# Reordering small copies, weight conversions and the mixing steps in a retention, softplus and SwiGLU kernel

## The chip, the cores and the metric

The kernel runs on one core of a Trainium2 chip. The metric is the time of one execution on the device in microseconds (us); lower is better. A core has five engines that run side by side, each through its own instructions in order: TensorE (PE in the rows; its weight loads are PEld), VectorE (DVE), ScalarE (ACT), GpSimd (POOL) and SyncE (SP, which issues most of the DMAs). An instruction that waits holds up everything behind it in its engine's queue, and nothing else.

## What is computed

```
state = gamma * state + k_t v_t^T ;  y_t = scale * q_t state        # retention, 2 x 8 heads, 768 steps, 64 wide
x  = y as [1536, 512]
h  = x @ w_in ; g = max(h, 0) + log1p(exp(-|h|)) ; x = g @ w_out     # 512 -> 2048 -> 512
rms = sqrt(mean(x * x) + 1e-6) ; xn = x / rms * rms_g
out = (silu(xn @ w_gate) * (xn @ w_val)) @ w_out2                    # 512 -> 1536 -> 512
```

Weights arrive as 64-bit floats and are read as pairs of 32-bit words. Every operand of a product is held as a high part (rounded) and a low part (the rest), and a product is three matmuls over these: high by high, high by low, low by high.

## The kernel before, in words

**Tiling.** The 1536 tokens are three blocks of 512, called 0, 1 and 2; block 2 is `LONE`. Features lie in tiles of 128. After retention come four groups of softplus layers: an `l1` piece makes one tile of h for a block (12 matmuls of 128 x 512), an `l2` piece adds one tile of the second layer (12 matmuls). In the last group the `l2` pieces of a block are followed by its norm: squares (ScalarE), sums over features (`sums`, VectorE), a mean by eight small matmuls and twelve small VectorE steps that give the root (`mean`), and four transposes with a ScalarE copy that lay the root along the tokens (`along`). For blocks 0 and 1 the normed x is then scaled (`scaled`) and split into high and low parts (`part`, `part_hi`, `part_lo`); block 2 is scaled only after its product, and its x parts are made by `high` and `low` in `norm`.

**Seven products.** The gate and value layers go in pairs of feature tiles, p = 0 to 5. Blocks 0 and 1 are multiplied together in seven products instead of eight (class `Seven`, p1 to p7, six matmuls each): x of both blocks is mixed into T1 to T4, B11, B21, B22 (`mixing`, eight steps of VectorE and ScalarE), and weights into two sums S (GpSimd, `combine` and `parts`). Bank Q collects p1, p6, p7 and p4, bank R p5 and p3. Between p1 and p6, p6 and p7, p7 and p4 ScalarE copies Q out (`copied`), since the partial value is wanted too; the next product into Q must wait for that copy. Block 2 has plain `l3` products (12 matmuls). Then Silu, the product of gate and value, its split (`to_g`: a high part on ScalarE, a low part on VectorE), and `l4` pieces (six matmuls) into the output.

**Order.** All is issued by hand, piece by piece. A piece's matmuls are issued first; then `piece(after, conv, us)` advances a planned clock by 2.72 or 1.36 us, runs what is due (`run`), what was deferred (`flush`, which also issues one weight load if a staging tile is free), as many conversions as asked, the piece's own `after`, and then one step each of two background lists, `bg` (sums, mean, along, plain, block after block) and `mix` (mixing). The planned clock decides only the order of the instructions. Pieces of the first pair come in the order: four `l2` pieces of block 2, then g.p1, g.p2, v.p1, v.p2 (g is the gate, v the value), four `l3` pieces, and the list of 14 that the last loop spells out. A round of p = 1 to 5 is four `l3` pieces alternating with four `l4` pieces (h0, L0, h1, L1, h2, L2, h3, L3), then two lists of eleven.

**Conversion of a weight tile** (`convert`): two ScalarE steps (`small`, `size`), two VectorE steps (`shift`, `bits`) and a GpSimd sum (`total`); later, by due times, `finish` (VectorE), `high` (ScalarE); for each second tile of gate and value also `combine` (four GpSimd steps), `whole` (two VectorE low parts), `parts` (two ScalarE high parts) and `rest` (two GpSimd low parts). `need` asks for a weight when its product is issued; were it not ready, all that is due would be run at once. There are 12 weight slots and three staging tiles.

## Time and profile before

| | us |
|---|---|
| median of three runs | 632.7 |
| the runs | 632.7, 2134.71, 631.86 |
| the profiled execution | 632.48 |
| its span (first to last instruction) | 630.8 |
| TensorE, VectorE, ScalarE, GpSimd busy | 605.5, 459.3, 355.5, 275.0 |
| granted TensorE clock, mean share | 0.992 |

The profile is of one execution. Busy time is the time with an instruction of that engine under way; 1.7 us of the execution lie outside the span. The granted clock is a share of 2.4 GHz.

### The profile page before, as it was taken

The numbers are of one execution on the slowest core, as the hardware profiler recorded it, in microseconds if no ns is written. First come the engines' busy times: TensorE is split into PE (matmuls) and PEld (weight loads), VectorE is DVE, ScalarE is ACT, GpSimd is POOL, SyncE is SP. The second block draws the span as 40 slices with busy tenths as digits, with TensorE's granted clock in tenths as the row PEclk, the third lists the DMA queues.
The fourth block names the chain that finished last, engine by engine and source line by source line (L and its number), as shares of the span: only waits on it lengthen the run. The fifth ranks groups of instructions, "written<-read, shape, count | busy, mean of one in ns | idle before, by whom it ended". The sixth has DMA issues, their size and how long they took to land.

```text
span 630.8 us, 8631 instructions
## 1 busy us (share of the span) xinstructions
PE 605.5 (96%) x3232; PEld 498.3 (79%) x3232; DVE 459.3 (73%) x655; ACT 355.5 (56%) x612; POOL 275.0 (44%) x228
## 2 busy tenths in 40 slices
PE   9999999999999999999897899899999999999997
PEld 8788888888888888887676678678878878878886
DVE  5787777678734774357879987489789789889735
ACT  3456677787746775566645564744444444543420
POOL 3444254544411442022321477277377377377211
PEclk9999999999999999999988999999999999999999
DMA  9997132333311331111100221211311212220014
GB/s 205 219 233 191 63 94 87 91 98 100 101 33 34 100 101 34 34 34 34 33 1 1 72 96 46 88 59 42 100 38 64 75 59 68 68 67 35 1 51 150
DMA packets 65562, 48.84 MB, mean 77 GB/s; under 512 B 39792, under 2 KB 60528, under 8 KB 65520
## 3 DMA queue, kind: packets, MB, share of 16 engines
q1 hardware_dynamic: 64320, 47.90, 26.9%
q8 instruction: 25, 0.41, 0.3%
q10 hardware_dynamic: 1200, 0.39, 0.2%
q14 instruction: 17, 0.14, 0.1%
HBM read 45.14 MB, written 3.15 MB: 77 GB/s over the span
## 4 chain that ended last, share of the span: by engine, by line
PE 57%; DVE 26%; ACT 8%; issue 4%; POOL 2%; SPq 2%; DMA 1%; DVEq 0%; POOLq 0%; ACTq 0%
PE h L483 18%; PE l L563 15%; PE l L885 6%; PE Q L787 5%; DVE g L765 4%; DVE w L200 3%; DVE a L258 3%; PE y L443 2%; DVE w L196 2%; PE R L787 2%; PE l L540 2%; PE sc L391 1%; DVE ws_w_gate L214 1%; SPq L84 1%; DVE ws_w_val L214 1%
## 5 line engine op out<-in xcount | busy, mean ns | idle before, releaser
L204 POOL TENSOR_TENSOR c<-w,c 128x512 uint32<-128x512 uint32 x68 | 87.8, 1291 | 169.1 <-DVE w L200 127.4
L483 PE MATMUL h<-x,ws_w_in 128*128 128x512 f32 x576 | 138.9, 391 | 0.0
L563 PE MATMUL l<-g,ws_w_out 128*128 128x512 f32 x528 | 129.8, 397 | 1.9 <-DVE g L125 1.9
L483 PEld LDWEIGHTS h<-x,ws_w_in 128*128 128x128 f32 x576 | 107.6, 188 | 22.9 <-issue 0.7
L563 PEld LDWEIGHTS l<-g,ws_w_out 128*128 128x128 f32 x528 | 101.2, 192 | 23.7 <-DVE g L125 2.2
L885 PE MATMUL l<-ws_w_out,g 128*128 128x512 f32 x432 | 109.3, 390 | 2.1 <-DVE g L765 2.1
L885 PEld LDWEIGHTS l<-ws_w_out,g 128*128 128x128 f32 x432 | 81.0, 188 | 20.0 <-DVE g L765 2.8
L521 DVE SCALAR_TENSOR_TENSOR t<-h,t 128x512 f32<-128x512 f32 x48 | 33.1, 690 | 73.9 <-ACT t L514 73.9
L214 POOL TENSOR_TENSOR ws_w_out<-a,ws_w_out 128x512 fp32r<-128x512 f32 x28 | 38.8, 1387 | 50.5 <-ACT ws_w_out L217 50.5
L258 DVE SCALAR_TENSOR_TENSOR a<-a,c 128x512 f32<-128x512 f32 x68 | 52.8, 776 | 9.3 <-POOL c L204 9.3
L124 ACT ACTIVATE g<-t 128x512 fp32r<-128x512 f32 x48 | 30.3, 632 | 37.2 <-DVE t L521 37.2
L765 DVE TENSOR_TENSOR g<-t,g 128x512 fp32r<-128x512 f32 x36 | 41.5, 1176 | 11.1 <-ACT g L764 8.2
L509 ACT ACTIVATE t<-h 128x512 f32<-128x512 f32 x48 | 28.6, 595 | 34.8 <-PE h L483 34.8
L125 DVE TENSOR_TENSOR g<-t,g 128x512 fp32r<-128x512 f32 x48 | 33.8, 707 | 13.0 <-ACT g L124 10.3
L214 POOL TENSOR_TENSOR ws_s<-s,ws_s 128x512 fp32r<-128x512 f32 x24 | 41.0, 1727 | 4.6 <-ACT ws_s L217 4.6
L808 POOL TENSOR_TENSOR t<-t,e 128x512 f32<-128x512 f32 x18 | 27.8, 1544 | 33.9 <-DVE e L804 33.9
L787 PE MATMUL Q<-T,ws_s 128*128 128x512 f32 x144 | 36.9, 394 | 2.7 <-ACT p L793 2.6
L764 ACT ACTIVATE g<-t 128x512 fp32r<-128x512 f32 x36 | 21.5, 624 | 28.6 <-DVE t L865 14.6
L483 PE MATMUL h_w_gate<-x,ws_w_gate 128*128 128x512 f32 x144 | 36.3, 403 | 0.0
L233 POOL TENSOR_TENSOR s<-a 128x256 f32<-128x256 f32 x24 | 21.3, 887 | 32.2 <-DVE a L258 32.2
L915 DVE TENSOR_TENSOR o<-l,o 128x512 f32<-128x512 f32 x39 | 26.6, 684 | 11.3 <-PE l L885 11.0
L787 PEld LDWEIGHTS Q<-T,ws_s 128*128 128x128 f32 x144 | 26.7, 188 | 10.2 <-ACT p L793 4.8
(132 smaller groups left out, 1041.2 us busy)
## 6 DMA issues: line engine op xcount, KB each, us to landing
st_w_out<-in_moe_w_out_dram SPq DMA_DIRECT2D x28, 512.0 KB, 3.4
st_w_in<-in_moe_w_in_dram SPq DMA_DIRECT2D x16, 512.0 KB, 3.8
st_w_gate<-in_moe_w_gate_dram SPq DMA_DIRECT2D x12, 512.0 KB, 3.6
st_w_val<-in_moe_w_val_dram SPq DMA_DIRECT2D x12, 512.0 KB, 3.5
v<-in_v_dram SPq DMA_DIRECT2D x12, 256.0 KB, 4.7
q<-in_q_dram SPq DMA_DIRECT2D x23, 128.0 KB, 4.4
k<-in_k_dram SPq DMA_DIRECT2D x23, 128.0 KB, 3.9
out_dram<-o SPq DMA_DIRECT2D x11, 256.0 KB, 2.0
```

The lines of the kernel that those rows point to most:

```text
L124: nc.scalar.activation(out=hi, in_=src, func=AF.Copy)
L125: eng.tensor_tensor(out=lo, in0=src, in1=hi.bitcast(F32), op=ALU.subtract)
L204: nc.gpsimd.tensor_tensor(out=c, in0=w, in1=c, op=ALU.add)
L214: eng.tensor_tensor(out=out[:, 1], in0=src, in1=out[:, 0].bitcast(F32), op=ALU.subtract)
L258: nc.vector.scalar_tensor_tensor(out=a, in0=a, scalar=TINY, in1=c.bitcast(F32), op0=ALU.is_ge, op1=ALU.mult)
L483: nc.tensor.matmul(h, lhsT=w[:, i, kk * P:(kk + 1) * P], rhs=src[j][kk // 2][:, kk % 2, :], start=(n == 0), stop=(n == 3 * KC - 1))
L509: nc.scalar.activation(out=got[0], in_=h, func=AF.Abs)
L521: nc.vector.scalar_tensor_tensor(out=t, in0=h, scalar=0.0, in1=t, op0=ALU.max, op1=ALU.add)
L563: nc.tensor.matmul(p, lhsT=w[:, i, m * P:(m + 1) * P], rhs=g_t[b, f][:, j, :], start=(n == 0 and f == (0 if keep else fs[0])), stop=(n == ...
L765: nc.vector.tensor_tensor(out=g[:, 1], in0=t, in1=g[:, 0].bitcast(F32), op=ALU.subtract)
L787: nc.tensor.matmul(ps, lhsT=halves(w[:, i], p)[:, kk * P:(kk + 1) * P], rhs=t[j][:, kk, :], start=start and n == 0, stop=n == 5, skip_grou ...
L885: nc.tensor.matmul(ps4, lhsT=g_t[b, f][:, j, m * P:(m + 1) * P], rhs=w[:, i, :], start=n == 0 and (i, j) == TERMS[0], stop=n == 1 and (i, ...
```

## The change

Four things are done. In p1, p6 and p7 the copy of Q becomes the piece's `first`, which `piece` runs ahead of everything else that it issues. The steps of a conversion get later due times, the two sums' tiles are taken in `combine`, and the calls of `convert` stand at other pieces. The last background step of block 0 (`plain`) becomes four, one feature tile each, and the two lists become a list of chains, of which each gives a step per piece: block 0's, block 1's, mixing (seven empty steps ahead), block 2's, in this order. Means and roots of blocks 1 and 2 stand one or two steps later, and the last list of the first pair puts each `l4` piece one place later.

```diff
@@ -207,7 +207,7 @@
         t = rows(slot[key], f"ws_{nm}")
         raw[key] = a
         if gated and f % 2:
-            sums, sa = [], [row(f"s{n}", "s") for n in range(2)]
+            sums, sa = [], []
             reserved[0] += 2
 
         def rounded(out=t, src=a, eng=nc.gpsimd):
@@ -224,6 +224,7 @@
         def combine():
             other = ws[nm, f - 1]
             a0, a1 = raw.pop((nm, f - 1)), a
+            sa.extend(row(f"s{n}", "s") for n in range(2))
             s1, s2 = (halves(sa[0], p) for p in range(2))
             s3, s4 = (halves(sa[1], p) for p in range(2))
             for out, x0, x1, op in ((s1, halves(a1, 0), halves(a1, 1), ALU.add),
@@ -251,7 +252,7 @@
                         rounded(out, sa[n])
                         ready.add(("S", nm, f // 2, n))
                 later(1.4, rest)
-            later(1.3, whole)
+            later(2.6, whole)
             later(4.0, parts)
 
         def finish():
@@ -259,13 +260,13 @@
                                            op0=ALU.is_ge, op1=ALU.mult)
             if not gated:
                 if nm == "w_out2":
-                    later(1.0, last)
+                    later(2.6, last)
                 else:
                     deferred.append(last)
             else:
-                later(1.0, high)
+                later(2.6, high)
                 if f % 2:
-                    later(0.9, combine)
+                    later(1.3, combine)
 
         ws[key] = t
         left[key] = 2 if gated else NB
@@ -284,7 +285,7 @@
         if nm in ("w_in", "w_out"):
             deferred.append(finish)
         else:
-            later(4.0, finish)
+            later(5.4, finish)
         return True
 
     def need(key):
@@ -472,7 +473,7 @@
 
     g_t, acc, tags = {}, {}, {}
     bg = []
-    mix = []
+    chains = []
     LONE = NB - 1
 
     def project(h, w, src):
@@ -636,17 +637,16 @@
             for do in waiting.pop(b, ()):
                 do()
 
-        def plain():
-            scaled(b, range(KC))
-            for m in range(KC):
-                part(("B11", "B21")[m // 2], m % 2, acc[b, m])
+        def plain(m):
+            scaled(b, (m,))
+            part(("B11", "B21")[m // 2], m % 2, acc[b, m])
 
         if m == KC - 1:
-            bg.extend(([None, sums, None, mean, None, along, plain],
-                       [None, sums, mean, along],
-                       [None, sums, None, mean, None, along])[b])
+            chains.append(([None, sums, None, mean, None, along] + [lambda m=m: plain(m) for m in range(KC)],
+                       [None, sums, None, mean, None, None, along],
+                       [None, None, None, sums, None, mean, along])[b])
             if b == 1:
-                mix.extend([None, None, None, None] + mixing())
+                chains.append([None] * 7 + mixing())
 
 
     TB, waiting = {}, {}
@@ -813,8 +813,12 @@
             self.Q = self.hold("Q")
             self.product(self.Q, (self.nm, 2 * self.p), 0, "B11", True)
 
+            def first():
+                self.c1 = self.copied(self.Q, "p1")
+
             def after():
-                self.c1 = self.copied(self.Q, "p1")
+                pass
+            after.first = first
             return after
 
         def p2(self):
@@ -837,17 +841,24 @@
             self.product(self.Q, key, 1, "T2", False)
             free.append(slot[key])
 
+            def first():
+                self.c6 = self.copied(self.Q, "p6")
+
             def after():
-                self.c6 = self.copied(self.Q, "p6")
+                pass
+            after.first = first
             return after
 
         def p7(self):
             self.product(self.Q, ("S", self.nm, self.p, 1), 0, "T3", False)
 
+            def first():
+                self.c7 = self.copied(self.Q, "p7")
+
             def after():
-                t, tag = self.copied(self.Q, "p7")
-                self.added(1, 1, self.R, t)
-                two.append(tag)
+                self.added(1, 1, self.R, self.c7[0])
+                two.append(self.c7[1])
+            after.first = first
             return after
 
         def p4(self):
@@ -922,17 +933,15 @@
 
     def piece(after, conv=1, us=2.72):
         clock[0] += us
+        if hasattr(after, "first"):
+            after.first()
         run()
         flush()
         for _ in range(conv):
             convert()
         after()
-        if bg:
-            step = bg.pop(0)
-            if step:
-                step()
-        if mix:
-            step = mix.pop(0)
+        for chain in chains:
+            step = chain.pop(0) if chain else None
             if step:
                 step()
 
@@ -1112,33 +1121,33 @@
             for n, one in enumerate([g.p1, g.p2, v.p1, v.p2]):
                 piece(one(), n == 1, half)
             for n, one in enumerate(h):
-                piece(one(), n in (1, 3))
+                piece(one(), n in (1, 2))
             later(0.4, gs_of(p, LONE))
             L = l4s(0, LONE)
-            for n, one in enumerate([g.p5, v.p5, g.p6, v.p6, L[0], g.p7, v.p7, L[1], g.p4, v.p4, L[2], g.p3, v.p3, L[3]]):
+            for n, one in enumerate([g.p5, v.p5, g.p6, v.p6, g.p7, L[0], v.p7, L[1], g.p4, L[2], v.p4, L[3], g.p3, v.p3]):
                 if n == 6:
                     later(0, lambda: to_g(0, 0))
                 if n == 11:
                     later(0, lambda: to_g(0, 1))
-                piece(one(), n in (2, 6, 10), half)
+                piece(one(), n in (0, 5, 9), half)
             continue
         L = l4s(p - 1, 0)
         for n in range(4):
             if n == 1:
                 later(0, gs_of(p - 1, 1))
-            piece(h[n](), n == 2)
-            piece(L[n](), n == 0, half)
+            piece(h[n](), n in (0, 2))
+            piece(L[n](), False, half)
         later(0, gs_of(p, LONE))
         L = l4s(p - 1, 1)
         for n, one in enumerate([g.p1, g.p2, g.p5, L[0], g.p6, L[1], g.p7, L[2], g.p4, L[3], g.p3]):
-            piece(one(), n in (3, 8), half)
+            piece(one(), n in (2, 6), half)
         L = l4s(p, LONE)
         for n, one in enumerate([v.p1, v.p2, v.p5, L[0], v.p6, L[1], v.p7, L[2], v.p4, L[3], v.p3]):
             if n == 4:
                 later(0, lambda: to_g(0, 2 * p))
             if n == 9:
                 later(0, lambda: to_g(0, 2 * p + 1))
-            piece(one(), n in (2, 7), half)
+            piece(one(), n in (0, 5), half)
     p = NPR - 1
     for b in (0, 1):
         for m, one in enumerate(l4s(p, b)):
```

## Rows read from the trace of the kernel before

**Rows 1.** The page, part 1: busy us (share of the span) xinstructions.

```profile
PE 605.5 (96%) x3232; PEld 498.3 (79%) x3232; DVE 459.3 (73%) x655; ACT 355.5 (56%) x612; POOL 275.0 (44%) x228
```

**Rows 2.** Windows: length, busy us of each engine (x instructions), granted clock, DMA share, GB/s.

```profile
302.47:373.50 71.03, 61.35 (x254) 48.34 (x252) 61.66 (x101) 40.78 (x72) 25.61 (x20) 0.93 0.12 38
373.50:424.78 51.28, 47.17 (x206) 38.07 (x204) 35.32 (x44) 28.79 (x53) 33.26 (x26) 1.00 0.20 63
424.78:473.18 48.40, 46.82 (x205) 38.15 (x204) 41.76 (x51) 22.85 (x41) 28.82 (x23) 1.00 0.21 66
...
569.98:616.25 46.27, 46.27 (x205) 38.31 (x204) 31.61 (x40) 17.07 (x29) 16.42 (x13) 1.00 0.08 28
```

**Rows 3.** Waits of TensorE: us in total, times, longest.

```profile
PE Q L787 <- ACT p L793: 9.6, 7, 1.8
```

**Rows 4.** Timeline of TensorE in round 1: start, us, instructions [idle before <-releaser].

```profile
397.18 1.66 PE L787 MATMUL Q<-T,ws_s 128*128 128x512 f32 x6 [1.76 <-ACT p L793]
...
420.55 1.65 PE L787 MATMUL Q<-T,ws_w_val 128*128 128x512 f32 x6 [1.54 <-ACT p L793]
...
424.78 2.88 PE L483 MATMUL h_w_gate<-x,ws_w_gate 128*128 128x512 f32 x12
```

**Rows 5.** Timeline of ScalarE in round 1.

```profile
394.49 0.63 ACT L217 ACTIVATE ws_w_out<-a 128x512 fp32r<-128x512 f32 x1 [1.77 <-DVE a L258]
...
396.55 0.58 ACT L793 ACTIVATE p<-Q 128x512 f32<-128x512 f32 x1
...
419.38 0.63 ACT L217 ACTIVATE ws_w_val<-a 128x512 fp32r<-128x512 f32 x1 [3.58 <-DVE a L258]
```

**Rows 6.** Timeline of TensorE in the first block.

```profile
302.47 7.94 PE L563 MATMUL l<-g,ws_w_out 128*128 128x512 f32 x34
312.33 5.07 PE L563 MATMUL l<-g,ws_w_out 128*128 128x512 f32 x14 [1.92 <-DVE g L125]
318.88 1.02 PE L617 MATMUL ms<-ones,sq 128*128 128x1 f32 x8 [1.47 <-DVE sq L612]
319.76 4.59 PE L563 MATMUL l<-g,ws_w_out 128*128 128x512 f32 x12
...
327.40 1.52 PE L787 MATMUL Q<-B,ws_w_gate 128*128 128x512 f32 x6
...
339.90 0.65 PE L633 MATMUL root<-ident,root_t 128*128 128x128 f32 x4 [3.23 <-DVE root_t L628]
...
344.72 5.62 PE L483 MATMUL h_w_val<-x,ws_w_val 128*128 128x512 f32 x24
...
357.67 0.96 PE L885 MATMUL l<-ws_w_out,g 128*128 128x512 f32 x3 [1.35 <-DVE g L765]
```

**Rows 7.** Timeline of VectorE in the first block.

```profile
305.94 2.73 DVE L658 SCALAR_TENSOR_TENSOR x<-x,rg,root 128x512 f32<-128x512 f32 x4
308.59 2.49 DVE L667 TENSOR_TENSOR B<-x,B 128x512 fp32r<-128x512 f32 x4
...
311.60 0.68 DVE L125 TENSOR_TENSOR g<-t,g 128x512 fp32r<-128x512 f32 x1
...
315.31 1.75 DVE L611 TENSOR_TENSOR sq<-sq 128x1024 f32<-128x1024 f32 x1
317.09 1.65 DVE L612 TENSOR_TENSOR sq<-sq 128x512 f32<-128x512 f32 x1
...
322.12 0.16 DVE L628 SCALAR_TENSOR_TENSOR root_t<-small,root_t 128x4 f32<-128x4 f32 x1
...
325.46 1.42 DVE L658 SCALAR_TENSOR_TENSOR x<-x,rg,root 128x512 f32<-128x512 f32 x2 [1.86 <-ACT root L634]
...
328.81 1.23 DVE L611 TENSOR_TENSOR sq<-sq 128x1024 f32<-128x1024 f32 x1
```

**Rows 8.** Windows of the first block: columns as in rows 2.

```profile
313.40:316.80 3.40, 3.40 (x10) 2.63 (x9) 3.40 (x4) 2.06 (x5) 3.40 (x4) 0.50 0.00 0
```

**Rows 9.** Timeline of GpSimd in the first block.

```profile
315.94 3.92 POOL L214 TENSOR_TENSOR ws_s<-s,ws_s 128x512 fp32r<-128x512 f32 x2
```

## Prediction, made before the change was run

> **What bounds the kernel now.** I read the page's engine line first, then busy time by stretch, then TensorE's own timeline for its gaps, and last the queues of the engine that each gap names. TensorE is busy 96% of the span [rows 1], so only its idle and its slow stretches can be won. The windows [rows 2] cut the last 314 us into the first block (the last six l2 pieces, the first pair p = 0) and the five rounds p = 1 to 5 that follow. Round 5, which has no conversions, takes 46.27 us with TensorE busy throughout: the floor of a round, 34 half pieces of 1.36 us. Rounds 2 to 4 take 48.40 each, 2.13 over it, round 1 51.28, 5.01 over it. The first block takes 71.03 with TensorE busy 61.35, and that at a granted share of 0.93; its pieces at full pace are 51.7 (12 + 26 half pieces of 1.36), so with means and roots some 54 would do: 17 us lie there. Before 302.47 no step of the change falls otherwise than now: with pieces of 2.72 us a due time of 4.0 or 5.4 is reached at the second piece, 1.0 or 2.6 or 0.9 or 1.3 at the first. Everything that can be won is 17 + 5 + 6.4 = 28 us.
>
> In rounds 1 to 4 the waits name ScalarE's copy p (9.6 us in 7 waits) [rows 3]: a product that accumulates in bank Q may not start before the copy of the product before it. In round 1 it starts at 420.55 after 1.54 idle [rows 4]. ScalarE's queue shows why [rows 5]: a conversion's high at 419.38 waited 3.58 for VectorE, and only behind it came the copy; in round 1 too the copy of p1 (0.58 long) ran behind such a high part. In the first block TensorE waits for g's low part (1.92), the square sums (1.47), the root (3.23) and g of block 2 (1.35 and more) [rows 6], and all of these are VectorE's. VectorE's queue from 305.94 on has next to no hole [rows 7]: there VectorE is the bound (61.66 busy of 71.03, [rows 2]), and TensorE waits where it has run ahead of it.
>
> Three times TensorE falls to half pace there: the granted clock is 0.50, 1.2 of 2.4 GHz, in the stretch from 313.4 [rows 8] and in two more like it, each after one of these waits. It costs 1.7 us each time: 12 matmuls last 4.59 [rows 6] instead of the 2.88 of 12 at full clock [rows 4].
>
> **Copies first.** Nothing is added; in p1, p6 and p7 the copy goes ahead of the due high parts, Silus, to_g parts and the conversion's two ScalarE steps of its own piece, though not ahead of what earlier pieces queued. In rounds 2 to 4, at v.p7, what stood ahead was w_val's high part, now due behind it twice over (copy first, finish at 5.4 and high 2.6 later). I count ScalarE's new queue from the end of v.p6: copy 0.58, to_g's copy and the conversion's two steps at the 0.63 of the high part [rows 5], so it is free some 2.6 us after, and v.p7 ends 2.72 after: the copy is done some 0.5 before the next product wants it. The 1.54 and its refill (a group of 6 after a stall lasts 1.65, [rows 4], 0.13 longer than without) go: 1.8 per round. The small rest of 2.13 is g.p6 to g.p7, where a Silu of the piece before still waits for VectorE; it may go or grow by 0.5. Cover: VectorE is busy 41.76 of 48.40, and must do the same in 46.5. **Three rounds: -5.4**, bounds -2.4 (VectorE binds) and -6.4 (floor).
>
> Who waits behind a copy that is now first: the highs, Silus and conversions of that piece, up to one piece (1.36 us) each. Their consumers have two to six pieces to spare by the new due times.
>
> **Conversions further apart.** No instruction more or less; six conversions a round, their calls now at h0, h2, g.p5, g.p7, v.p1 and L1 of the last list. I walked the due times: with 46.24 us a round the gate's pair is converted at 20.40 and 25.84, finished at 25.84 and 31.28, whole by 35.36, wanted at 48.96; the value's pair is whole at 48.96, its sums at 53.04, wanted at 54.40 and later. Slots never run out (the fewest free is one at h2 and at g.p5, and one is what a conversion asks). So no weight comes late, and loads, one per free staging tile, move by at most two pieces. Cost 0.
>
> **Round 1.** Of its 5.01, 1.8 is the same v.p7 wait, and 3.2 are the two at g.p6 and g.p7: at g.p6 TensorE starts at 397.18 after 1.76 idle [rows 4]; the copy of p1 ran at 396.55 behind a high part that had waited 1.77 for VectorE at 394.49 [rows 5]. First in its own piece, and with that high part due three half pieces later, it can run by about 394; p6's copy still has a Silu ahead of it that depends on VectorE. I leave 1.5 standing: **-3.5**, bounds -1 and -5.
>
> **First block: four parts, means and roots later.** The work is the same; the order is new, and VectorE is in order. In turn:
> (a) Now VectorE scales four pieces and then takes four low parts, 2.73 + 2.49 without a hole [rows 7], while ScalarE makes the high parts beside it. One piece a step is scale, high part (0.63 on ScalarE, the form of row 419.38 [rows 5]), low part, in series: VectorE stands some 0.7 us in each of four steps, for the next instruction in its queue is the low part itself. But g's low part (311.60, ended 312.28) then stands behind one pair and a finish, not four pairs: ended about 309.3, and TensorE asks for it at about 310.2, in the 34th matmul after 302.47 [rows 6]. The 1.92 and the first half-clock stretch go.
> (b) Block 1's square sums (315.31, ended 318.74) come behind all four pairs, at about 320.7 by the same rows, 2 later. The mean's matmuls are one piece later; without a stall TensorE gets there at 316.1 (302.47 + five pieces of 2.72). It waits some 4.7 instead of 1.47, and half clock must be feared after that. Then 1.02 for the mean's matmuls, 2.72 for the last l2 piece and about 1 of half clock: g.p1 starts near 325.6 instead of 327.40 [rows 6], -1.8.
> (c) Mixing starts behind block 1's root, which is two pieces later: near 330.8 instead of 325.46 [rows 7]. In the new lists mixing's steps stand before block 2's in every piece. So between 330.8 and the end of block 2's mean VectorE has: four scales 2.8 (two take 1.42 at 325.46), four differences 2.5 (at a low part's 0.62), block 2's sums 1.9 (1.23 and a plain 0.68), an addition 0.7, two low parts 1.2, a finish 0.7, the mean's twelve small steps 2.3 (the last ends at 322.28, the matmuls of the mean at 319.90) [rows 6, 7], together 12.1, and about 2.5 behind GpSimd's instructions: near 345.6. TensorE, which has one l3 piece more behind it by then, waits some 4 us; the next piece starts at 346.2, where it now starts at 344.72 [rows 6]. Plus 1 to 2 of half clock.
> (d) ScalarE's six high parts of mixing's sixth step (3.6 us) and g of block 2 now fall right before the copies of p6; g.p7 waits some 2 for that, where now L0 waits 2.1 for g. L0 itself, one piece later, should find its g (now TensorE starts on it again at 357.67).
> Sum: **+1.5** for the block. Bounds: -8 (of the present waits only the root's stays: -1.9 - 1.5 - 1.4 and two half clocks) and +8 (the waits of b, c and d as computed and 1.7 of half clock behind each).
>
> **VectorE against GpSimd.** The two sums of squares take 1.75 and 1.65 us at 315.31, while GpSimd runs two subtractions in 3.92 from 315.94 [rows 9], and 1.23 for the first of the same form at 328.81, where GpSimd, done at 319.86, runs nothing [rows 7]. So moving VectorE's work among GpSimd's doesn't shorten the pair's sum. The Trainium skill, page "SBUF — State Buffer", section "SBUF: two separate sides", says that the pair of ports which VectorE's two-input operations and GpSimd share is an exclusive lock held for a whole instruction; the trace's 1.75 against 1.23 agrees. Were the ports shared evenly, (b) would come about 1.5 earlier and the block out even; I keep the lock.
>
> **Sum.** 632.48 (span 630.8 and 1.7 around it; the median of the runs shown is 632.7) - 5.4 - 3.5 + 1.5 = 625.1: **625 us**.
>
> **Rivals.** *The block gains as well*: the chains in parallel let VectorE catch up, the sums are ready when TensorE comes, two half-clock stretches vanish: -8 instead of +1.5, so 616. For it: 17 us of waiting lie in this block, five steps are moved away from the places that wait now. Against: VectorE has no hole to catch up in [rows 7].
> *The copies are first, but of their own piece only, and VectorE takes the bound*: what earlier pieces queued on ScalarE waits for VectorE, busy 41.76 of 48.40 and locked against 28.8 of GpSimd; the v.p7 wait moves to g.p7. Rounds -2.4, round 1 -2, block +4: 632, no change. For it: at 394.49 a ScalarE instruction of an earlier piece was what waited. Against: round 2's own copy at g.p7 is late by only 0.3.
> *Block 2's root behind mixing* (slower): one mechanism, one place, (c). If VectorE reaches that mean at 350 and not 345.6, TensorE idles 8 there, falls to half clock for two stretches, and every later copy of the block comes late by the same: block +13, against -8.9 elsewhere, so 637. It decides from a block over +9 on.
>
> **How the numbers follow.** Forecast 0.50 (own range 619 to 630), block gains too 0.22, no change 0.20, slower 0.08. The range takes in most of the first two rivals and half of the last's way up: 615 to 634. A measurement of this kernel tells about 2% from no change (below 620.0, above 645.4): faster 0.24 (nearly all of the first rival, the forecast's edge), same 0.73, slower 0.03.
>
> **What would show it.** Right: rounds 2 to 4 between 46.3 and 47.2, the copy at v.p7 ahead of w_val's high part; no wait for g's low part at 310; a wait of 4 to 5 before block 1's mean and of about 4 before block 2's root; the block near 72.5. Wrong: the mean's matmuls start by 317, or the root's wait is under 2 (then the block gains); or TensorE still waits over 1 us for a copy in each round.

## The result and the profile after

| | us |
|---|---|
| before, median of four runs | 632.65 |
| after, median of four runs (626.33 to 627.75) | 626.87 |
| ratio, 95% interval | 0.9914 (0.9895 to 0.9934) |
| the profiled execution after, its span | 626.81, 625.1 |

The ratio leaves out the one run of 2134.71 us before. The changed kernel is 0.9% faster, inside the forecast's own range (619 to 630), 1.9 us over its 625; being under 2%, it counts as "same" among the prediction's chances (0.73). The first look goes to the engine line: TensorE's and VectorE's busy times have hardly moved from [rows 1], so the difference is again one of idle and of clock.

```profile
PE 602.5 (96%) x3232; PEld 499.0 (80%) x3232; DVE 450.8 (72%) x655; ACT 354.3 (57%) x613; POOL 277.2 (44%) x228
```

Then the windows of the same stages, with the columns of [rows 2]: the first block, round 1, round 2 (rounds 3 and 4 are as long as round 2), and below them two stretches within the first block.

```profile
302.22:378.34 76.12, 61.08 (x253) 49.01 (x252) 61.41 (x99) 41.12 (x74) 25.89 (x20) 0.89 0.11 35
378.34:425.59 47.25, 46.56 (x206) 38.22 (x204) 36.30 (x48) 29.00 (x53) 33.91 (x27) 1.00 0.25 78
425.59:471.83 46.24, 46.24 (x206) 38.29 (x204) 39.31 (x52) 22.44 (x41) 29.14 (x24) 1.00 0.21 69
319.00:329.20 10.20, 7.11 (x21) 5.98 (x22) 6.86 (x17) 2.56 (x5) 2.39 (x2) 0.50 0.01 2
346.30:353.10 6.80, 3.79 (x11) 3.22 (x12) 6.39 (x19) 1.83 (x3) 1.60 (x1) 0.50 0.22 72
```

Against [rows 2] this is +5.09 for the block (76.12 - 71.03), -4.03 for round 1, -2.16 for each of rounds 2 to 4, and -0.25 ahead of the block: -5.67, which is the difference of the spans (625.1 - 630.8 = -5.7). Rounds 2 to 4 stand on their floor, TensorE busy in all of 46.24. The block got longer, and its granted clock fell from 0.93 to 0.89: two stretches at half pace of 10.2 and 6.8 us stand where three of 3.4 stood.

TensorE's waits (us in total, times, longest) say what changed places. Copies, the longest entry in [rows 3] with 9.6 us, are down to 1.7; the sums of squares and the root lead.

```profile
PE ms L618 <- DVE sq L613: 8.2, 2, 6.1
PE root L634 <- DVE root_t L629: 5.9, 2, 5.4
PE Q L787 <- ACT p L793: 1.7, 2, 1.0
PE l L896 <- POOL ws_w_out L214: 0.5, 1, 0.5
```

TensorE's timeline of the first block, the counterpart of [rows 6]:

```profile
302.22 13.76 PE L564 MATMUL l<-g,ws_w_out 128*128 128x512 f32 x60
322.09 1.84 PE L618 MATMUL ms<-ones,sq 128*128 128x1 f32 x8 [6.11 <-DVE sq L613]
323.79 5.47 PE L564 MATMUL l<-g,ws_w_out 128*128 128x512 f32 x12
329.05 1.63 PE L787 MATMUL Q<-B,ws_w_gate 128*128 128x512 f32 x6
...
340.00 1.05 PE L618 MATMUL ms<-ones,sq 128*128 128x1 f32 x8 [2.05 <-DVE sq L613]
...
349.31 1.12 PE L634 MATMUL root<-ident,root_t 128*128 128x128 f32 x4 [5.38 <-DVE root_t L629]
350.07 7.15 PE L484 MATMUL h_w_val<-x,ws_w_val 128*128 128x512 f32 x24
...
363.70 1.66 PE L787 MATMUL Q<-T,ws_s 128*128 128x512 f32 x6 [1.04 <-ACT p L793]
```

The wait for g at 312 is gone (60 matmuls run through), but the mean of block 1 is waited for 6.11 us, and everything behind it runs at half pace to 329.2: 12 matmuls in 5.47.

VectorE and GpSimd in the same stretch, the counterparts of [rows 7, 9]. Of the four low parts (L667) three show the wait for ScalarE's high part as 0.70, the last as 0.69:

```profile
307.15 0.69 DVE L667 TENSOR_TENSOR B<-x,B 128x512 fp32r<-128x512 f32 x1 [0.70 <-ACT B L664]
...
308.36 0.68 DVE L125 TENSOR_TENSOR g<-t,g 128x512 fp32r<-128x512 f32 x1
...
317.36 0.69 DVE L667 TENSOR_TENSOR B<-x,B 128x512 fp32r<-128x512 f32 x1 [0.69 <-ACT B L664]
317.97 2.30 DVE L612 TENSOR_TENSOR sq<-sq 128x1024 f32<-128x1024 f32 x1
320.31 1.64 DVE L613 TENSOR_TENSOR sq<-sq 128x512 f32<-128x512 f32 x1
...
332.42 0.75 DVE L605 SCALAR_TENSOR_TENSOR x<-l,rg,x 128x512 fp32r<-128x512 f32 x1 [4.79 <-ACT sq L601]
```

```profile
317.93 3.47 POOL L214 TENSOR_TENSOR ws_s<-s,ws_s 128x512 fp32r<-128x512 f32 x2 [5.18 <-ACT ws_s L217]
```

The last VectorE row is a hole of 4.79 us, a wait for the squares of block 2. ScalarE can make these only behind the copy of g.p1, which now stands first and had to wait for its own product:

```profile
330.72 0.60 ACT L793 ACTIVATE p<-Q 128x512 f32<-128x512 f32 x1 [9.16 <-PE Q L787]
```

And ScalarE at v.p7 of round 2: the copy waits only for its own product, and the high part comes behind it, as the change wants it.

```profile
466.59 0.60 ACT L793 ACTIVATE p<-Q 128x512 f32<-128x512 f32 x1 [0.43 <-PE Q L787]
467.08 0.62 ACT L217 ACTIVATE ws_w_val<-a 128x512 fp32r<-128x512 f32 x1
```

From these traces alone each step for the rounds seems to do what was foreseen. The experiments say otherwise.

### The profile page after: what moved, and what is told of

Read it like the earlier page. It is cut to its first block, busy times and chain, and to the rows that moved or that the text cites. A ratio compares the mean times of both kernels' runs of the same rounds, so it can differ in the third digit from the quotient of the medians.

```text
span 625.1 us, 8622 instructions
## 1 busy us (share of the span) xinstructions
PE 602.5 (96%) x3232; PEld 499.0 (80%) x3232; DVE 450.8 (72%) x655; ACT 354.3 (57%) x613; POOL 277.2 (44%) x228
## 4 chain that ended last, share of the span: by engine, by line
PE 76%; DVE 13%; ACT 7%; issue 2%; POOL 1%; DMA 1%; SPq 0%; DVEq 0%; POOLq 0%
PE h L484 17%; PE l L564 15%; PE l L896 13%; PE Q L787 9%; PE R L787 4%; PE h_w_val L484 3%; PE h_w_gate L484 3%; PE y L444 2%; PE sc L392 2%; PE W L787 2%; PE l L541 2%; PE pt L373 1%; DVE x L658 1%; DVE T L667 1%; DVE g L125 1%
## 5 line engine op out<-in xcount | busy, mean ns | idle before, releaser
L204 POOL TENSOR_TENSOR c<-w,c 128x512 uint32<-128x512 uint32 x68 | 90.0, 1324 | 159.8 <-DVE w L200 133.3
L564 PE MATMUL l<-g,ws_w_out 128*128 128x512 f32 x528 | 128.4, 395 | 0.0
L793 ACT ACTIVATE p<-Q 128x512 f32<-128x512 f32 x36 | 21.3, 596 | 68.0 <-PE Q L787 68.0
L259 DVE SCALAR_TENSOR_TENSOR a<-a,c 128x512 f32<-128x512 f32 x68 | 50.7, 746 | 7.1 <-POOL c L204 7.1
L124 ACT ACTIVATE g<-t 128x512 fp32r<-128x512 f32 x48 | 30.3, 631 | 37.2 <-DVE t L522 37.2
L765 DVE TENSOR_TENSOR g<-t,g 128x512 fp32r<-128x512 f32 x36 | 35.2, 1002 | 17.8 <-ACT g L764 17.8
L214 POOL TENSOR_TENSOR ws_s<-s,ws_s 128x512 fp32r<-128x512 f32 x24 | 39.1, 1650 | 9.8 <-ACT ws_s L217 9.8
L125 DVE TENSOR_TENSOR g<-t,g 128x512 fp32r<-128x512 f32 x48 | 33.9, 707 | 13.0 <-ACT g L124 10.3
L484 PE MATMUL h_w_val<-x,ws_w_val 128*128 128x512 f32 x144 | 36.0, 401 | 0.0
L484 PE MATMUL h_w_gate<-x,ws_w_gate 128*128 128x512 f32 x144 | 34.7, 390 | 0.0
L234 POOL TENSOR_TENSOR s<-a 128x256 f32<-128x256 f32 x24 | 24.2, 1007 | 23.5 <-DVE a L259 23.5
```

Of the source, the lines that this page charges most:

```text
L124: nc.scalar.activation(out=hi, in_=src, func=AF.Copy)
L125: eng.tensor_tensor(out=lo, in0=src, in1=hi.bitcast(F32), op=ALU.subtract)
L204: nc.gpsimd.tensor_tensor(out=c, in0=w, in1=c, op=ALU.add)
L214: eng.tensor_tensor(out=out[:, 1], in0=src, in1=out[:, 0].bitcast(F32), op=ALU.subtract)
L259: nc.vector.scalar_tensor_tensor(out=a, in0=a, scalar=TINY, in1=c.bitcast(F32), op0=ALU.is_ge, op1=ALU.mult)
L484: nc.tensor.matmul(h, lhsT=w[:, i, kk * P:(kk + 1) * P], rhs=src[j][kk // 2][:, kk % 2, :], start=(n == 0), stop=(n == 3 * KC - 1))
```

## The experiments

The theory: the copies in front take the waits out of the rounds, the spacing of the conversions costs nothing, and the first block loses by VectorE's order. The main rival: the spacing is what clears ScalarE's queue, and the place of the copies matters little. The change was cut into five parts: the *first copies*; the *due times* of a conversion (with them the tiles of the two sums, taken in `combine`); the *places* of its calls in the rounds; the *chains* (parts by tile, means and roots later); the *list* (the first pair's last 14 pieces and its places). Stages are measured on TensorE: the block from the first transposes of block 0's root, a round from its first l3 product to the next round's. So measured the block is 3 us longer than the window above. Every kernel ran four times or more beside the kernel before (its medians: 632.95, 633.12 and 633.62 on the three chips used).

| kernel | block | round 1 | rounds 2 to 4, each | median | ratio (95%) |
|---|---|---|---|---|---|
| before | 74.29 | 51.28 | 48.40 | 632.65 | 1 |
| after (all five) | 79.37 | 47.25 | 46.24 | 626.87 | 0.9914 (0.9895-0.9934) |
| e1: first copies | 78.31 | 50.69 | 50.65, 50.67, 49.03 | 643.97 | 1.0165 (1.0126-1.0203) |
| e2: due times, places | 75.04 | 48.14 | 46.24 | 621.96 | 0.9833 (0.9795-0.9872) |
| e3: after without chains | 79.31 | 46.24 | 46.24 | 625.46 | 0.9873 (0.9834-0.9912) |
| e4: after, block 2 ahead of mixing | 78.48 | 47.25 | 46.24 | 625.96 | 0.9885 (0.9853-0.9918) |
| e6: after, parts by tile overlapped | 75.75 | 47.25 | 46.24 | 621.19 | 0.9817 (0.9781-0.9853) |
| f1: e2 + first copies from p = 1 on | 73.48 | 48.29 | 46.24 | 622.76 | 0.9841 (0.9814-0.9869) |
| f2: e2 + first copies | 77.77 | 49.27 | 46.24 | 626.60 | 0.9900 (0.9870-0.9930) |
| f3: e2 + chains | 80.32 | 46.68 | 46.24 | 627.79 | 0.9915 (0.9888-0.9942) |
| g1: due times | 75.84 | 46.26 | 47.0 | 623.63 | 0.9844 (0.9827-0.9862) |
| g2: places | 75.87 | 48.73 | 46.3 | 624.44 | 0.9856 (0.9842-0.9871) |
| h1: e3, no first copies at p = 0 | 76.79 | 46.24 | 46.24 | 623.32 | 0.9840 (0.9823-0.9856) |
| h2: e6, old positions, no first copies at p = 0 | 78.37 | 46.24 | 46.24 | 625.02 | 0.9869 (0.9852-0.9885) |

The start of the block moves by 1 to 2 us between kernels (298.8 to 301.7), so parts of the block are compared by stage, not by the total. The stages come from one profiled execution each, which need not be near the median: in e2 and e6 it was the slowest of four (625.03 and 622.97).

**e1, the first copies alone.**

```diff
     def piece(after, conv=1, us=2.72):
         clock[0] += us
+        if hasattr(after, "first"):
+            after.first()
         run()
```

> The kernel before with nothing but the copies of p1, p6 and p7 first in their pieces. If the copies carry the gain of the rounds: rounds 2 to 4 at 46.3 us instead of 48.40, round 1 at 47 to 49 instead of 51.28, the first block within 2 us of 71.0, about 622 in all. If the spacing of the conversions carries it (the copy still waits for what an earlier piece queued): rounds 2 to 4 above 47.5 and about 630 in all.

It is 1.65% slower than before: the second case, and 14 us worse than the 630 expected of it. At v.p7 of round 2 the copy does come as soon as its product ends:

```profile
475.61 0.60 ACT L793 ACTIVATE p<-Q 128x512 f32<-128x512 f32 x1 [0.50 <-PE Q L787]
```

But the wait did not vanish, it moved from v.p7 to g.p7, and TensorE's clock falls behind it (round 2 has a share of 0.97). TensorE's timeline at g.p7 of round 2:

```profile
457.32 2.39 PE L787 MATMUL Q<-T,ws_s 128*128 128x512 f32 x6 [1.89 <-ACT p L793]
```

ScalarE's timeline ahead of that copy shows why, e1 first and the same instructions of the kernel before behind it:

```profile
446.93 0.66 ACT L190 ACTIVATE c<-st_w_out 128x512 uint32<-128x512 uint32 x1
...
451.25 0.63 ACT L217 ACTIVATE ws_w_out<-a 128x512 fp32r<-128x512 f32 x1 [3.10 <-DVE a L258]
451.78 0.58 ACT L793 ACTIVATE p<-Q 128x512 f32<-128x512 f32 x1
...
455.04 0.63 ACT L801 ACTIVATE t<-t 128x512 f32<-128x512 f32 x1 [1.64 <-DVE t L800]
...
456.70 0.57 ACT L793 ACTIVATE p<-Q 128x512 f32<-128x512 f32 x1
```

```profile
439.05 0.67 ACT L190 ACTIVATE c<-st_w_out 128x512 uint32<-128x512 uint32 x1
...
443.37 0.64 ACT L217 ACTIVATE ws_w_out<-a 128x512 fp32r<-128x512 f32 x1 [3.09 <-DVE a L258]
...
447.16 0.64 ACT L801 ACTIVATE t<-t 128x512 f32<-128x512 f32 x1 [1.64 <-DVE t L800]
...
448.85 0.57 ACT L793 ACTIVATE p<-Q 128x512 f32<-128x512 f32 x1
```

From a conversion's first step to p6's copy ScalarE takes 9.77 us in e1 (456.70 - 446.93) and 9.80 before (448.85 - 439.05), with the same two waits for VectorE, 3.1 and 1.64. A copy that is first in its piece still stands behind what earlier pieces queued, and that waits for VectorE. TensorE only comes to it earlier: g.p1 starts 0.07 after that first step in e1 (at 447.00), and 2.05 after it in the kernel before (at 441.10).

**e2, the spacing alone** (due times and the rounds' places; nothing is first, chains and list as before).

```diff
-            later(4.0, finish)
+            later(5.4, finish)
...
-                later(1.0, high)
+                later(2.6, high)
...
-            piece(one(), n in (3, 8), half)
+            piece(one(), n in (2, 6), half)
```

> The kernel before with nothing but the later due times of the conversions and their new places in the rounds; copies, first pair's order and mixing steps as before. If the copies carry the gain: rounds 2 to 4 stay at 48 or more, about 631. If the spacing alone takes the blocked high part out of the copy's way (it is due one piece later and its finish is done by then): rounds 2 to 4 at 46.3 to 46.8, about 626. The two parts would then be two ways to the same 6 us and not add up.

1.7% faster, 4 us better than the 626 expected: rounds 2 to 4 are on the floor without any copy in front. At v.p7 of round 2 ScalarE still runs the high part ahead of the copy, and it does no harm, since it no longer waits for VectorE:

```profile
464.02 0.63 ACT L217 ACTIVATE ws_w_val<-a 128x512 fp32r<-128x512 f32 x1
464.82 0.60 ACT L794 ACTIVATE p<-Q 128x512 f32<-128x512 f32 x1 [0.16 <-PE Q L788]
```

e1 and e2 together reject the theory's first step and bear out the rival. The copies in front are not a second way to the same gain, as the expectation had it.

**g1 and g2, the spacing in its two halves**: only the due times (the first two pairs of lines of e2's diff and the other `later` calls), only the places (the last pair, with those of the other lists of a round).

> The kernel before with only the later due times of the conversions; their places stay. The value's even tile, converted at v.p5, then has its finish due at v.p7 and its high part at v.p4, behind the copy of p7. If that is what frees the copy: no wait at v.p7, rounds 2 to 4 at 46.3 to 46.8 us, and a rest at g.p7, where the conversion's ScalarE steps still stand before p6's copy: up to 2. If the places are what counts: rounds of 48 or more.

> The kernel before with only the new places of the conversions in rounds 1 to 5; due times as before. The value's even tile is then converted at v.p1 and its high part due at v.p6, one piece list earlier than the copy of p7. If places are what frees the copies: rounds 2 to 4 at 46.3 to 46.8. If the high part now blocks the copy of p6 instead: a wait of 0.5 to 2 at v.p7 or g.p7 and rounds of 47 to 48.4.

The places alone give nearly all of it (46.3), the due times alone two thirds (47.0, with a wait of 0.45 left at g.p7), in two ways. ScalarE's waits for `finish` in rounds 2 to 4 (us, times, longest), of before, of g1 and of g2 in turn:

```profile
ACT ws_w_val L217 <- DVE a L258: 16.8, 6, 3.6
...
ACT ws_w_out L217 <- DVE a L258: 10.5, 6, 3.1
```

```profile
ACT ws_w_val L217 <- DVE a L259: 2.1, 3, 0.7
...
ACT ws_w_out L217 <- DVE a L259: 0.8, 3, 0.3
```

```profile
ACT ws_w_val L217 <- DVE a L258: 16.3, 6, 3.3
...
ACT ws_w_out L217 <- DVE a L258: 8.9, 6, 2.1
```

Later due times take the 27.3 us of waiting out of ScalarE's queue (2.9 left); new places leave 25.2 of it and put it where the copy behind it still comes in time: no wait of TensorE for a copy shows in these rounds of g2.

**f1, f2, f3: e2 with one part more.** f1 adds the first copies from p = 1 on, f2 in the first pair too, f3 adds the chains.

```diff
+        first = getattr(after, "first", lambda: None)
+        if upto[0]:
+            first()
         run()
...
+        if not upto[0]:
+            first()
         after()
```

(f1; `upto` holds p. f2 has the lines of e1, f3 those of the change.)

> Spacing alone (the kernel of the run with only that) plus copies first in rounds 1 to 5, not in the first pair; background steps and the first pair's order as before. If the spacing carries the rounds and copies first only help where ScalarE's queue is still blocked: rounds 2 to 5 at 46.24 as with spacing alone, round 1 at 46.3 to 47 instead of 48.14, the block (from block 0's root transposes to round 1's first product) at 75, about 620 to 621 in all. If copies first hurt wherever they stand, round 1 is no shorter than 48.1.

> Spacing plus copies first everywhere, background steps and the first pair's order as before. If copies first in the first pair are what costs the block: it takes 77 us or more (75.0 with spacing alone, 79.3 with copies, spacing and the new list of the first pair), about 623 to 624. If the new list of l4 pieces and conversions is what costs: 75 to 76, about 620 to 621.

> Spacing plus the new chains of background steps, without copies first and with the first pair's old list. If the chains cost the block by themselves: 78 us or more instead of 75.0, about 625. If they cost only together with copies first (which hold block 2's squares behind g.p1): 75 to 77, about 622 to 623. If they gain once the copies are gone: under 74, about 620.

f1's rounds are e2's: with the spacing there, the first copies do nothing in them, not in round 1 either (48.29, where 46.3 to 47 was the hope). f2's block is 4.3 longer than f1's. Of that 1.5 lie ahead of g.p1, where both issue the same and only the granted clock differs (last section); 2.7 lie behind it, as against e2. In the first pair a copy in front is a loss, and the medians of the two say so too (626.60 and 622.76). ScalarE's timeline at g.p1 of f2 (first fence) and of f1 (second):

```profile
330.38 0.60 ACT L794 ACTIVATE p<-Q 128x512 f32<-128x512 f32 x1 [2.45 <-PE Q L788]
330.88 0.68 ACT L599 ACTIVATE x<-l,rg 128x512 fp32r<-128x512 f32 x1
```

```profile
327.43 0.69 ACT L599 ACTIVATE x<-l,rg 128x512 fp32r<-128x512 f32 x1 [1.09 <-PE l L564]
...
328.79 0.60 ACT L794 ACTIVATE p<-Q 128x512 f32<-128x512 f32 x1 [0.18 <-PE Q L788]
```

The copy waits 2.45 for its product, and the norm of block 2 (L599) stands behind it: it runs 2.06 after g.p1's start (328.82), in f1 0.20 after it (327.23). VectorE then stands 1.90 for block 2's squares in f2, and not at all in f1.

f3's block is 5.3 longer than e2's (waits 6.09 for block 1's sums and 5.39 for block 2's root, against 6.11 and 5.38 after): the chains alone are enough for a loss of the block's size. Up to block 2's root f3 issues what the changed kernel does, but for the place of the copies. Without them VectorE's hole of 4.79 is 2.07:

```profile
331.20 0.75 DVE L605 SCALAR_TENSOR_TENSOR x<-l,rg,x 128x512 fp32r<-128x512 f32 x1 [2.07 <-ACT sq L601]
```

The root's transposes then start 18.29 after g.p1, in the changed kernel 20.26: the first copies cost 2.0 there.

**e3 and h1: the change without the chains.** e3 puts `bg` and `mix` back, h1 also takes the first copies out of the first pair.

```diff
-            chains.append(([None, sums, None, mean, None, along] + [lambda m=m: plain(m) for m in range(KC)],
...
+            bg.extend(([None, sums, None, mean, None, along, plain],
...
-                chains.append([None] * 7 + mixing())
+                mix.extend([None, None, None, None] + mixing())
```

> The changed kernel with the background steps of the kernel before: two lists, block 0 in one step, means, roots and mixing where they stood. If the new order of these steps costs the block 5 us: the block (six l2 pieces and the first pair) returns to 69 to 71 us from 76.1, the rounds stay at 46.2 to 47.3, about 621 in all. If the new order is not what costs (the copies put first in the first pair are): the block stays above 74 and the time near 627.

> Spacing, the new list of the first pair, background steps as before, copies first from round 1 on only. Against the run with old chains and copies first everywhere it takes the copies out of the first pair: if they cost the block there, it falls from 79.3 to 75 or less; if the new list is what costs, it stays at 78 or more. Round 1 at 46.2, rounds at 46.24, about 619 to 620 in all if the block falls.

Taking the chains out does not shorten the block: e3's is as long as the changed kernel's, where 69 to 71 was expected if the chains cost it 5 us. So the chains are enough for the loss (f3), and copies and list are enough without them (e3); the two don't add up. h1 falls between its two cases, and of the 2.5 that its block is shorter than e3's 1.5 lie ahead of g.p1, where only the clock differs.

Round 1 goes to its floor, 46.24, in both, from 48.29 in f1. f1 and h1 differ only in the list, so the list does this; whether by its order or by its earlier conversions was not run. The block stays long for another reason: the list wants p6's copy one piece sooner, and g.p7 waits for it (from g.p1 on h1's block is 3.3 longer than f1's). TensorE of e3, then of h1:

```profile
363.13 2.92 PE L788 MATMUL Q<-T,ws_s 128*128 128x512 f32 x6 [5.68 <-ACT p L794]
```

```profile
360.96 2.93 PE L788 MATMUL Q<-T,ws_s 128*128 128x512 f32 x6 [4.11 <-ACT p L794]
```

**e4: block 2's chain ahead of mixing.** This aims at step (c), by which block 2's mean waits behind mixing.

```diff
-            chains.append(([None, sums, None, mean, None, along] + [lambda m=m: plain(m) for m in range(KC)],
+            chains.insert(len(chains) - (b == LONE), ([None, sums, None, mean, None, along] + [lambda m=m: plain(m) for m in range(KC)],
```

> The changed kernel with block 2's sums, mean and root ahead of mixing's step in each piece, not behind it. If mixing ahead of them is what keeps TensorE waiting 5.38 us for the root: that wait falls under 2 us, one half-clock stretch goes with it, and the time falls by 4 to 6 us to about 622. If VectorE's whole load is the bound there, the wait comes back later (before p6 or p7, or at the l4 piece) and the time stays within 1 us of 626.9.

The root is waited for 5.19 instead of 5.38, and the copy of p6 then 2.52 instead of 1.04:

```profile
346.48 1.11 PE L634 MATMUL root<-ident,root_t 128*128 128x128 f32 x4 [5.19 <-DVE root_t L629]
...
363.17 1.65 PE L787 MATMUL Q<-T,ws_s 128*128 128x512 f32 x6 [2.52 <-ACT p L793]
```

Counted from g.p1, the root's transposes start 2.61 earlier (17.65 instead of 20.26), and the wait of 2.05 before block 2's mean is gone, so TensorE comes to the root earlier as well. The time is handed on: the 24 products behind the root take 7.97 instead of 7.15, for they have more of half clock, and the copy of p6 stands behind high parts of mixing that wait 2.66 for VectorE instead of 1.57. The order of the two doesn't set the block.

**e6: the four parts overlapped**, so that VectorE never stands for ScalarE's high part: a step scales tile m, and takes the low part of tile m - 1.

```diff
         def plain(m):
-            scaled(b, (m,))
-            part(("B11", "B21")[m // 2], m % 2, acc[b, m])
+            if m < KC:
+                scaled(b, (m,))
+                part_hi(("B11", "B21")[m // 2], m % 2, acc[b, m])
+            if m:
+                part_lo(("B11", "B21")[(m - 1) // 2], (m - 1) % 2, acc[b, m - 1])
```

> The changed kernel with block 0's parts in five steps, each with the scale and high part of one tile and the low part of the tile before, so that VectorE need not wait for ScalarE between them. If that wait makes block 1's sums late: TensorE's wait before block 1's mean falls from 6.11 to 3 to 4.5 us and the time by 2 to 3 us. If the order of the work is the cause and not the wait: it stays near 6 and the time near 626.9.

The block is 3.6 shorter than after's, the wait for block 1's sums 2.73 instead of 6.11:

```profile
318.47 1.84 PE L618 MATMUL ms<-ones,sq 128*128 128x1 f32 x8 [2.73 <-DVE sq L613]
```

Block 1's sums end 19.57 after the block's start, as in the kernel before (19.53), in the changed kernel 22.97. So the parts in series cost this much, their clock included. Not all of it is the four waits of 0.70 (2.8 together): the edit also puts the last low part behind the sums, and the first sum takes 1.22 instead of 2.30, with GpSimd starting 0.74 behind it and not beside it. The wait fell below the 3 to 4.5 expected, and the time by 5.7 (medians) instead of 2 to 3. The median, 621.19, is the lowest of the study; e2's, 621.96, lies within its interval. Both beat the kernel before and the changed one.

**h2: h1 with overlapped parts, parallel chains in their old positions, block 2 ahead of mixing.** It combines what e4 and e6 did for the block.

```diff
+            chains.insert(len(chains) - (b == LONE),
+                          ([None, sums, None, mean, None, along] + [lambda m=m: plain(m) for m in range(KC + 1)],
+                           [None, sums, mean, along],
+                           [None, sums, None, mean, None, along])[b])
```

> As the run before it in this call, with block 0's parts in five overlapped steps and the chains in parallel, block 2 ahead of mixing, every mean, root and mixing step at its place of the kernel before. If the wait between VectorE and ScalarE and the later places are all that the new chains cost, g's low part is no longer waited for (1.93 gone) and the rest stays: block 71 to 74, about 617 to 619. If VectorE's load is the bound: the wait moves to the mean or the root and the block stays at 74 to 75.

A miss: the block lasts 78.37. No wait for g is left, but TensorE waits 5.45 for the sums, 3.23 for the root and 4.06 for p6's copy. In h1 the first two were 1.92 for g and 1.49 for the sums. The sums end at the same time in both, 19.57 and 19.52 after the block's start: VectorE has the same work up to there, so the wait for g came back as a wait for the sums. The block is 1.58 longer, 1.54 of it ahead of g.p1: behind the sums half clock lasts some 6.8 us in h2 and 3.4 in h1, which had another 3.4 before them, where TensorE would have waited anyway.

## Why the prediction was right, and where it was not

**The total came out in the range, in part by luck: two of its terms have their causes exchanged, and the rounds' gain (1.6 more than foreseen in all) hides part of the block's loss (3.6 more).** *Copies first* (-5.4 in rounds 2 to 4) came out as -6.48 (3 x 2.16), near its floor bound of -6.4, and at v.p7 the trace shows the very order foreseen. But the term fails: alone the edit makes these rounds 0.6 to 2.3 longer (e1), and on top of the spacing it does nothing (f1 against e2). The count of ScalarE's queue "from the end of v.p6" held: in e1 the copy of p7 is done at 476.21, 0.56 before the next product (476.77), and some 0.5 was foreseen. (Its 1.54 and 0.13 add to 1.67, not 1.8; by the starts of the products the stall before was 1.69 and 0.13.) What failed is the sentence on the rest, that g.p7 "may go or grow by 0.5". In e1's round 4, at full clock throughout, g.p7 starts 2.05 behind an unbroken sequence, against 0.21 before: it grows by 1.84, all that v.p7 gives back. The second rival had the mechanism ("what earlier pieces queued on ScalarE waits for VectorE ... moves to g.p7"); e1 shows it to the place. What was held against it, that the copy at g.p7 was late by only 0.3, was the margin of a TensorE which had just been held up at v.p7; with that wait gone, it comes 2 us sooner.

**"Conversions further apart. Cost 0" failed**, on the good side. It counted slots, due times and late weights, rightly but for one wait of 0.46 for a low part at L0 of the first pair, and not the 27.3 us that ScalarE stands waiting for `finish` in rounds 2 to 4. The row was at hand ([rows 5], the 3.58 at 419.38): the prediction saw that the new due times put it behind the copy, but took them for a second safeguard, and not for what removes the wait. e2 and g1 show that taking the wait away brings the rounds' gain, g2 that moving it away from the copies does so too.

**Who waits behind a first copy failed in the first pair.** The prediction gave all of them "two to six pieces to spare", and the block's sum has nothing for it. Block 2's norm, behind g.p1's copy, had none to spare: f2 against f1 has 2.7 us behind g.p1, f3 against the changed kernel 2.0 at block 2's root.

**Round 1**: -3.5 foreseen, -4.03 measured, one wait of 0.69 left. Its cause too is not the copies: the due times alone bring the round to 46.26 (g1), the places give 1.9 of it back (48.14 in e2), and the new list takes that away again (46.24 in e3 and h1).

**First block**, +1.5 foreseen, +5.09 measured; nearly all of the miss is one term.
- (a) held: VectorE stands 0.70 in each of four steps, g's low part ends at 309.04 (309.3), no wait at 310 and no half clock there.
- (b) was mis-sized. TensorE came at 315.98 (316.1) and waited 6.11, not 4.7; the sums started 2.66 later than before and took 2.30 + 1.64 beside GpSimd's 3.47, so they ended 3.2 later, not 2. Half clock behind it took some 3.5, not 1 (from 322.09 to 329.2 at half pace). So g.p1 started at 329.05, not 325.6: 3.45 of the block's 3.6 too much, 1.3 by the sums and 2.2 by half clock. The four waits of 0.70 themselves were foreseen in (a).
- (c) was right in size: VectorE took 14.50 from mixing's start (334.75) to the root's end (349.25), without a hole, where 14.6 was foreseen. All of it came late, since (b) passed 3.45 on, so the next piece starts at 350.07 and not at 346.2. TensorE waited 5.38 for the root (some 4) and 2.05 before block 2's mean, which the sum does not have. Mixing ahead of block 2 does hold the root up, by 2.61 (e4), but taking it away shortens the block by only 0.9, and the wait for the root stays. VectorE's work is the bound from 332.42 to the root; ahead of that it stands idle for the 4.79, of which the first copy makes more than half (2.07 in f3).
- (d) held in place, 1.04 at g.p7 instead of 2, and L0 found its g (it waited 0.46 for a weight).

The bounds of the block (-8 to +8) held it, and the range the total. The first rival, a gain in the block, did not come true in any of the twelve kernels (the shortest block, f1's, is 0.8 under before's, less than the clock alone can make). The slower rival did not either: its point was a block over +9.

**VectorE against GpSimd**: the rows fit the lock that the prediction kept. The two sums of block 2, without GpSimd, take 1.21 and 0.69; those of block 1, beside GpSimd's 3.47, take 2.30 and 1.64. Both grow by about the same time, 1.09 and 0.95, and not by the same factor. An exclusive lock held for a whole instruction, as the Trainium skill has it (page "SBUF — State Buffer", section "SBUF: two separate sides"), agrees with that. No run tests it by itself.

**Left open**: why the waits of e1's rounds come out larger than those they replace. In round 4, at full clock, g.p7 takes 1.84 more than before and v.p7 1.82 less; p6 of the gate and p3 of the value lose 0.6 more between them, the latter by a wait of 0.17 for VectorE. That is all of 49.03 against 48.40, but what sets the new waits is not shown. e2 with e6's parts, and e2 with the list alone, were not run.

## What to carry to other kernels

When a small instruction on an in-order queue is late, look first at what the instruction ahead of it waits for, and issue that one later or its producer earlier; putting the small one in front of its own group leaves it behind all that earlier groups queued, and moves the wait to the next place. What is put behind it must then wait for its product. When a batch is cut into single steps between two engines, let each step finish the step before, or the batch pays a wait per step. A gain in a trace of several edits says nothing of which edit made it: run each alone before keeping it.

## What the runs showed of the hardware

Half clock was dearer than foreseen. The three waits of 1.5 to 3.2 us before had 3.4 us at a share of 0.50 behind each [rows 8]; after, the stretch that began within the 6.11 us wait lasted 10.2, and the one within the 5.38 us wait 6.8. Nor is it the same where the same instructions are issued: up to g.p1, f1 and e2 differ in nothing, and yet g.p1 starts 28.18 after the block's start in one and 29.77 in the other, with 12 products behind the same wait of 3.1 taking 4.60 and 5.38. And the wait of 1.92 for g, behind which 14 products took 5.07 before [rows 6], is 1.93 in e2, and there the 14 run at full clock, in TensorE's timeline:

```profile
313.76 3.46 PE L564 MATMUL l<-g,ws_w_out 128*128 128x512 f32 x14 [1.93 <-DVE g L125]
320.31 1.83 PE L618 MATMUL ms<-ones,sq 128*128 128x1 f32 x8 [3.08 <-DVE sq L613]
322.01 5.38 PE L564 MATMUL l<-g,ws_w_out 128*128 128x512 f32 x12
```

Differences of up to 1.6 us between blocks of single profiles are therefore not read as effects here.
